# A fused attention and token-mixing kernel: when the queries and keys of two batches are loaded

## The chip, the cores and the metric

The kernel runs on one core of a Trainium2 chip. A core has a matrix engine (TensorE, in the profile PE, with its weight loads as PEld), a vector engine (VectorE, DVE), an activation engine (ScalarE, ACT), GpSimd (POOL) and SyncE (SP). GpSimd, SyncE and ScalarE also issue transfers, which a set of 16 DMA engines carries out. The metric is the device time of one execution in microseconds (us).

## The reference, cut to what matters

Four batches of attention (8 heads, 768 tokens, 64 channels a head) with a band of 96 local tokens and 8 global ones, followed by a layer that mixes tokens and channels. Everything is float32.

```python
# attention, per batch b and head h
scores = (q @ k.T) / sqrt(64) + bias      # bias: -slope_h * distance
scores = where(is_global | is_local, scores, -1e9)
a = softmax(scores)
x[b, :, h*64:(h+1)*64] = a @ v            # x is (4, 768, 512)
# the layer behind it, per batch
theta = x @ w_theta
zr, zi = x * cos(theta), x * sin(theta)
y = w_tok_r @ zr + w_tok_i @ zi           # over the 768 tokens
u = x + y
out = u + maximum(u @ w_ch, 0)
```

## The kernel before

The queries q, keys k and values v are loaded by GpSimd's queue, which also casts them to bfloat16. A buffer `qk` holds the q and k of one batch; there are two such buffers, so batch 3 takes the one that batch 1 leaves. The same holds for `vn` and v.

```python
ld = ctx.enter_context(tc.tile_pool(name="ld", bufs=2))
...
def alloc_qk(b):
    loads[b] = [ld.tile([T, 2, H, NT, D], BF, name="qk"), None]

def load_qk(b, h0, n, which=(0, 1)):           # rows of 6 tokens x 64 channels
    qk = loads[b][0]
    for i_ in which:
        nc.gpsimd.dma_start(
            out=qk[:, i_, h0:h0 + n].rearrange("p h t d -> p h (t d)"),
            in_=(q, k)[i_][b, h0:h0 + n].rearrange("h (p t) d -> p h (t d)", p=T))

def load_qk_tokens(b, h0, n):                  # one piece per head and tensor
    qk = loads[b][0]
    for h in range(h0, h0 + n):
        for i_ in range(2):
            pair = qk[:, i_, h // 2 * 2:h // 2 * 2 + 2].rearrange("p h t d -> p (h t d)")
            nc.gpsimd.dma_start(
                out=pair.rearrange("p (t h d) -> p t h d", t=NT, h=2)[:, :, h % 2],
                in_=(q, k)[i_][b, h].rearrange("(t p) d -> p t d", p=T))
```

Batches 0 to 2 are loaded by `load_qk`; batch 3 by `load_qk_tokens`, in an order in which a transposing DMA can turn a pair of heads without a copy ahead of it. Batches 1 and 2 need such a copy on VectorE and transposes on TensorE:

```python
def prep_copy(b, p):                           # batches 1 and 2
    ...
    with behind("dve"):
        for i_ in range(2):
            nc.vector.tensor_copy(
                out=qkn[:, :, i_].rearrange("p t h d -> p h t d"), in_=qk[:, i_, 2 * p:2 * p + 2])

def prep_dma(b, p):                            # batch 3: k and q of one pair of heads
    ...
    for i_ in (1, 0):
        to = qkT[(b, p)][i_] = att.tile([T, S], BF, name=("qT", "kT")[i_], bufs=6)
        with behind("sp"):
            nc.sync.dma_start_transpose(
                out=to.rearrange("p (t s) -> p t s", t=NT),
                in_=qk[:, i_, 2 * p:2 * p + 2].rearrange("p h t d -> p (h t d)"))
```

SyncE's queue carries three kinds of work in the order of the program: these transposes, the transposes of the attention's output x (`xtrans`) and of u (`utrans`) from batch 1 on, and the outputs (`chan`). `kglob` copies parts of a transposed k to `kG` on VectorE. The weights and the loads behind them:

```python
def load_w():
    nc.gpsimd.dma_start(out=w_theta_bf, in_=moe_w_theta.rearrange("(c p) n -> p c n", p=T))
    for tt in range(0, NT, 2):                 # NT = 6
        for wi, src in enumerate((moe_w_tok_r, moe_w_tok_i)):
            w2 = moe.tile([T, 2, S], BF, name="w_nat", bufs=6)
            nc.gpsimd.dma_start(
                out=w2, in_=src[tt * T:(tt + 2) * T, :].rearrange("(a p) s -> p a s", p=T))
            w_nat[wi, tt], w_nat[wi, tt + 1] = w2[:, 0], w2[:, 1]
        if tt == NT - 4:
            load_all_qk(1)
    nc.gpsimd.dma_start(out=w_ch_bf, in_=moe_w_ch.rearrange("(c p) n -> p c n", p=T))

def load_behind(b, tile):                      # called for batch 3 at the start of batch 1's layer
    g = nc.gpsimd.tensor_copy(out=gate, in_=tile).ins
    with tc.issue_after(g):
        alloc_qk(b)
        load_qk_tokens(b, 0, H)
        load_all_v(b)
...
load_w()
load_all_v(1)
load_all_qk(2)
```

The attention of batch b + 1 is woven into the token mixing of batch b, a step of `side` after so much of `main`:

```python
for b in range(B):
    ...
    if b == 2:
        order[:0] = [lambda p=p: prep_dma(3, p) for p in range(1, NP)]
    if b == 1:
        order.insert(0, lambda: load_behind(3, xT_sb[1][0:1, NC - 1, 0:1]))
    ...
    side = [(1536, f) for f in pre]            # pre: the preparation of batch 1, for b == 0
    if b == 0:
        side[:0] = [(0, lambda: load_all_v(2))]
        pass
    side += attention_steps(nxt, ahead) if nxt else []
    weave(main, side, 0.3 if b == 0 else 0.0, 0.9)
```

From the end of batch 0's attention on, the instructions of one engine are put in order by a scheduler, save where `behind` or a manual part fixes it.

Of the kernel before, what the change touches and what calls it, by code (L numbers as in the profile page):

```python
# [16 lines left out]
def kernel(  # L17
# [14 lines left out]
    B, H, S, D = q.shape  # L32
    T = 128
    NT = S // T
# [28 lines left out]
    def alloc_qk(b):  # L63
        loads[b] = [ld.tile([T, 2, H, NT, D], BF, name="qk"), None]

    def alloc_v(b):
        vn = loads[b][1] = ld.tile([T, H, NT, D + 1], BF, name="vn")
        nc.vector.memset(vn[:, :, :, D:D + 1], 1.0)  # L68

    def load_qk(b, h0, n, which=(0, 1)):  # L70
# [6 lines that stand above are left out]
    def load_qk_tokens(b, h0, n):  # L77
# [8 lines that stand above are left out]
    def load_v(b, h0, n):  # L86
        vn = loads[b][1]
        nc.gpsimd.dma_start(out=vn[:, h0:h0 + n, :, 0:D].rearrange("p h t d -> p (h t) d"),  # L88
                            in_=v[b, h0:h0 + n].rearrange("h (t p) d -> p (h t) d", p=T))
# [63 lines left out]
    def load_w():  # L153
        nc.gpsimd.dma_start(out=w_theta_bf, in_=moe_w_theta.rearrange("(c p) n -> p c n", p=T))
        for tt in range(0, NT, 2):
            for wi, src in enumerate((moe_w_tok_r, moe_w_tok_i)):
                w2 = moe.tile([T, 2, S], BF, name="w_nat", bufs=6)
                nc.gpsimd.dma_start(
                    out=w2, in_=src[tt * T:(tt + 2) * T, :].rearrange("(a p) s -> p a s", p=T))
                w_nat[wi, tt], w_nat[wi, tt + 1] = w2[:, 0], w2[:, 1]  # L160
            if tt == NT - 4:
                load_all_qk(1)
        nc.gpsimd.dma_start(out=w_ch_bf, in_=moe_w_ch.rearrange("(c p) n -> p c n", p=T))

    def trans_w(tt, copy=nc.vector.tensor_copy):
# [70 lines left out]
    def prep(b, p):  # L236
        if p == 0:
            prep_copy(b, 0)
        if p + 1 < NP:
            prep_copy(b, p + 1)  # L240
        qkn = qkns[b, p]
        qT = att.tile([T, S], BF, name="qT", bufs=6)
        kT = att.tile([T, S], BF, name="kT", bufs=6)
        for i_, dst in ((0, qT), (1, kT)):
            ps = ps_small([T, NT, T], BF)
            with behind("pe"):
                for t_ in range(NT):
                    nc.tensor.transpose(ps[:, t_, :], qkn[:, t_, i_].rearrange("p h d -> p (h d)"), ident)  # L248
            dst = dst.rearrange("p (n t) -> p n t", t=NT)
            src = ps.rearrange("p t n -> p n t")  # L250
            if i_ == 0:
                nc.vector.tensor_copy(out=dst, in_=src)  # L252
            else:
                nc.scalar.copy(out=dst, in_=src)

        qkT[(b, p)] = [qT, kT, None]
        kglob(b, p)

    def prep_dma(b, p):
        qk = loads[b][0]  # L260
        qkT[(b, p)] = [None, None, None]
# [6 lines that stand above are left out]
# [117 lines left out]
    def theta(b, c, j):  # L385
        last0 = [(j_, NC - 1) for j_ in range(2)]
        part = {0: [(0, dc) for dc in range(NC - 1)],
                1: [(1, dc) for dc in range(NC - 1)] + last0,
                2: [(j_, dc) for j_ in range(2) for dc in range(NC - 1)],
                3: last0}[j]  # L390
        if c == 0 and j in (0, 2):
            zri[b] = moe.tile([T, 2, NT, DM], BF, name="zri", tag="zri", bufs=1)
        xT, xb = xT_sb[b], x_sb[b]
        last = c == NT // 2 - 1
        if j in (0, 2):
            pss["th", c] = [ps_small([T, DM], FP) for _ in range(2)] if last else ps_big()
        pb = pss["th", c]
        st = lambda j_: slice((2 * c + j_) * T, (2 * c + j_ + 1) * T)
        for j_, dc in part:
            nc.tensor.matmul(pb[j_] if last else pb[:, j_, :], lhsT=xT[:, dc, st(j_)],  # L400
                             rhs=w_theta_bf[:, dc, :], start=(dc == 0), stop=(dc == NC - 1))
        if j in (1, 3):
            cs = moe.tile([T, 2, 2, DM], BF, name="cs")
            for i_, bias in ((0, {"bias": halfpi}), (1, {})):
                for o, p_ in [(cs[:, i_, j_], pb[j_]) for j_ in range(2)] if last else [(cs[:, i_], pb)]:
                    nc.scalar.activation(o, p_, AF.Sin, **bias)  # L406
            for i_ in range(2):
                for j_ in range(2):
                    nc.vector.tensor_mul(  # L409
                        zri[b][:, i_, 2 * c + j_, :].rearrange("p (g d) -> p g d", g=NP),  # L410
                        xb[:, :, 2 * c + j_, :],
                        cs[:, i_, j_].rearrange("p (g d) -> p g d", g=NP))
# [45 lines left out]
    def load_all_qk(b):  # L458
        alloc_qk(b)
        load_qk(b, 0, 8)  # L460

    def load_all_v(b):
        alloc_v(b)
        load_v(b, 0, 8)
# [4 lines left out]
    def load_behind(b, tile):  # L469
        g = nc.gpsimd.tensor_copy(out=gate, in_=tile).ins  # L470
        with tc.issue_after(g):
            alloc_qk(b)
            load_qk_tokens(b, 0, H)
            load_all_v(b)

    def attention_steps(b, preps):
# [25 lines left out]
    def weave(main, side, s0=0.0, s1=1.0):  # L502
# [11 lines left out]
        while i_ < len(side):  # L514
            side[i_][1]()
            i_ += 1

    load_w()
    load_all_v(1)
    load_all_qk(2)  # L520
    alloc_x(0)
# [80 lines left out]
    for b in range(B):  # L602
        nxt = b + 1 if b + 1 < B else None
        lag = 3
        th = [lambda c=c, j=j: theta(b, c, j) for c in range(NT // 2) for j in range(2)]
        pre = [lambda p=p: prep(1, p) for p in range(NP)] if b == 0 else []
        ahead = [[lambda p=p: prep(2, p) for p in range(NP)], [lambda p=p: prep_dma(3, p) for p in range(1)],
                 [], []][b]
        order = rest[:1] + th[:4] + rest[1:2] + th[4:] + rest[2:] if b else []
# [4 lines that stand above are left out]
        for f in order:  # L614
            f()
        main = []
        for tt in range(NT):
            for g in range(NT // 2):
                if (b, tt) != (B - 1, NT - 1):
                    main.append((2048, lambda tt=tt, g=g: mix(b, tt, g)))  # L620
                if b == 0 and g == 1 and tt + 1 < NT:
                    main.append((1536, lambda tt=tt: trans_w(tt + 1)))
                if tt >= lag and g == 0 and (b, tt) != (B - 1, NT - 1):
                    main.append((2048, lambda tt=tt: chan(b, tt - lag)))
                if b == 0 and tt and g == 1:
                    main.append((512, lambda tt=tt: utrans(b, tt - 1)))
            if b and (b, tt) != (B - 1, NT - 1):
                main.append((0, lambda tt=tt: utrans(b, tt)))
        side = [(1536, f) for f in pre]
        if b == 0:  # L630
            side[:0] = [(0, lambda: load_all_v(2))]
            pass
        side += attention_steps(nxt, ahead) if nxt else []
        weave(main, side, 0.3 if b == 0 else 0.0, 0.9)
        rest = [lambda tt=tt, b=b: chan(b, tt) for tt in range(NT - lag, NT)]
        if b == 0:
            rest.insert(1, lambda b=b: utrans(b, NT - 1))
# [44 lines left out]
```

The softmax here doesn't subtract the row's maximum and nothing guards it: scores larger than these inputs give would overflow.

## Time and profile before

| | us |
|---|---|
| time, median of three runs | 177.21 |
| lowest and highest | 177.1 and 177.56 |
| span of the profiled execution | 175.5 |
| TensorE busy | 160.7 |
| VectorE busy | 125.7 |
| ScalarE busy | 99.3 |
| GpSimd's DMA queue, share of 16 engines' span | 79.0% |
| SyncE's DMA queue, share of 16 engines' span | 33.5% |

The page divides the span into 40 slices of 4.39 us and gives each engine's busy share of a slice as a digit in tenths; the row named DMA is the mean of the 16 DMA engines. A row of waits reads: engine and line that waited, what ended the wait, the total in us, how often, the longest. A row of a timeline reads: start and duration in us, engine, line, operation, output and input, how many in a row. L12 is line 12 of the kernel. Busy time of TensorE is modelled from pipelined products, so a full row doesn't mean that it works at its peak.

### The profile page before, as it was taken

The page shows a single profiled execution, that of the slowest core. Times are in us where ns is not written, and L with a number is a line of the kernel's source. Part 1 is how long each engine was busy: PE and PEld are TensorE (multiplying, and loading weights), DVE is VectorE, ACT ScalarE, POOL GpSimd, SP SyncE. Part 2 cuts the span into 40 slices and gives each one's busy share as a digit, 9 for nine tenths or more (in the row PEclk, how much of TensorE's full clock was granted, in tenths as well). Part 3 has the DMA queues.
Part 4 walks back from the last instruction along what each step waited for, and adds up shares of the span by engine and source line. Part 5 has one row for each costly group of instructions (what it writes and reads, how often), then busy time and mean ns, then how long its engine had stood idle before and what let it go on. Part 6 is the DMA issues. An engine that isn't in the chain of part 4 may idle for free.

```text
span 175.5 us, 3752 instructions
## 1 busy us (share of the span) xinstructions
PE 160.7 (92%) x1534; PEld 83.9 (48%) x1534; DVE 125.7 (72%) x286; ACT 99.3 (57%) x127; POOL 38.0 (22%) x45
## 2 busy tenths in 40 slices
PE   7489789899999999999999996889999999999991
PEld 2355455345756566544455552333554644444440
DVE  5737676678999999997768786088877865724442
ACT  4698583999497694389933810669545508500010
POOL 8965346005000000299940000000000000000000
PEclk9999999999999999999999999999999999999999
DMA  5999999999999942399999997878254384314335
GB/s 154 198 172 179 213 204 203 207 206 166 168 204 166 150 119 49 105 133 163 176 129 151 94 240 171 147 134 227 76 105 106 91 147 124 120 37 107 99 90 181
DMA packets 75089, 25.94 MB, mean 148 GB/s; under 512 B 63168, under 2 KB 72128, under 8 KB 75072
## 3 DMA queue, kind: packets, MB, share of 16 engines
q0 software_dynamic: 45680, 12.45, 79.0%
q1 hardware_dynamic: 28976, 12.72, 33.5%
q10 hardware_dynamic: 416, 0.52, 0.9%
q8 instruction: 12, 0.20, 0.5%
q14 instruction: 5, 0.04, 0.1%
HBM read 25.69 MB, written 6.29 MB: 182 GB/s over the span
## 4 chain that ended last, share of the span: by engine, by line
PE 56%; DVE 17%; ACT 10%; DMA 9%; POOL 3%; issue 2%; SPq 1%; DVEq 0%; ACTq 0%; POOLq 0%
PE ps L420 27%; PE ps L448 9%; DMA vn<-in_v_dram 7%; ACT cs L406 6%; PE pb L400 6%; PE pb L357 4%; PE pb L298 3%; POOL qk L73 2%; ACT e L308 2%; DMA kT<-qk 2%; DVE qT L252 2%; PE ps L400 2%; DVE e L317 2%; DVE x_sb L368 2%; PE ps L248 2%
## 5 line engine op out<-in xcount | busy, mean ns | idle before, releaser
L420 PE MATMUL ps<-zri,w_tokT 128*128 128x512 bf16 x288 | 71.2, 379 | 1.6 <-DVE zri L409 0.7
L308 ACT ACTIVATE e<-pb 128x1024 bf16<-128x1024 f32 (+1 forms) x48 | 43.6, 959 | 20.6 <-PE pb L298 20.1
L420 PEld LDWEIGHTS <-w_tokT 128*128 128x128 bf16 x288 | 26.1, 98 | 30.4 <-issue 2.6
L425 DVE TENSOR_TENSOR u<-x_sb,ps 128x512 bf16<-128x512 bf16 x24 | 16.4, 682 | 13.1 <-PE ps L420 13.1
L448 PE MATMUL ps<-w_ch_bf,uT 128*128 128x512 bf16 (+1 forms) x100 | 24.7, 371 | 0.0
L409 DVE TENSOR_TENSOR zri<-x_sb,cs 128x512 bf16<-128x512 bf16 x48 | 18.1, 420 | 5.2 <-ACT cs L406 4.8
L406 ACT ACTIVATE cs<-pb,halfpi 128x1024 bf16<-128x1024 f32 x8 | 8.9, 1115 | 21.0 <-PE pb L400 21.0
L453 DVE SCALAR_TENSOR_TENSOR o_sb<-ps,u 128x512 f32<-128x512 f32 (+1 forms) x25 | 16.5, 665 | 3.1 <-PE ps L448 3.1
L400 PE MATMUL pb<-w_theta_bf,xT 128*128 128x512 bf16 x64 | 15.5, 379 | 2.2 <-DMA xT<-x_sb 2.2
L298 PE MATMUL pb<-qT,kT 64*128 64x128 bf16 x224 | 15.7, 219 | 1.9 <-DVE qT L213 1.3
L317 DVE TENSOR_TENSOR e<-e,etab 128x1024 bf16<-128x1024 bf16 (+1 forms) x24 | 14.7, 616 | 3.6 <-ACT e L308 3.5
L298 PEld LDWEIGHTS <-kT 64*128 64x128 bf16 x224 | 9.1, 93 | 15.3 <-issue 12.6
L400 PEld LDWEIGHTS <-xT 128*128 128x128 bf16 x96 | 9.0, 98 | 13.1 <-DMA xT<-x_sb 3.6
L439 ACT COPY uT<-ps 128x512 bf16<-128x512 bf16 x7 | 4.1, 587 | 18.6 <-PE ps L438 18.6
L357 PEld LDWEIGHTS <-e 128*128 128x128 bf16 x352 | 12.7, 97 | 3.9 <-issue 1.7
L448 PEld LDWEIGHTS <-uT 128*128 128x128 bf16 x100 | 9.2, 98 | 10.0 <-ACT uT L439 0.8
L298 PE MATMUL pb<-qT,kG 64*128 64x128 bf16 x128 | 12.0, 217 | 0.7 <-DVE kG L224 0.4
L88 POOL DMA_DIRECT2D vn<-in_v_dram x5 | 9.7, 1940 | 12.0 <-DVE vn L68 10.3
L368 DVE TENSOR_TENSOR x_sb<-pb,rec 128x768 bf16<-128x768 f32 x12 | 11.4, 949 | 0.3
L320 DVE TENSOR_TENSOR e<-e,etab 128x1024 bf16<-128x1024 bf16 x12 | 8.2, 685 | 2.9 <-ACT e L308 2.9
L222 DVE COPY kG<-kT 128x512 bf16<-128x512 bf16 x15 | 4.2, 282 | 8.0 <-DMA kT<-qk 5.8
L357 PE MATMUL pb<-vn,e 128*128 128x65 bf16 x168 | 9.6, 193 | 0.0
(73 smaller groups left out, 204.9 us busy)
## 6 DMA issues: line engine op xcount, KB each, us to landing
out_dram<-o_sb SPq DMA_DIRECT2D x23, 256.0 KB, 2.4
vn<-in_v_dram POOLq DMA_DIRECT2D x3, 768.0 KB, 22.3
qk<-in_q_dram POOLq DMA_DIRECT2D x2, 768.0 KB, 21.0
qk<-in_k_dram POOLq DMA_DIRECT2D x2, 768.0 KB, 24.0
w_nat<-in_moe_w_tok_r_dram POOLq DMA_DIRECT2D x3, 384.0 KB, 15.6
w_nat<-in_moe_w_tok_i_dram POOLq DMA_DIRECT2D x3, 384.0 KB, 15.1
vn<-in_v_dram POOLq DMA_DIRECT2D x2, 384.0 KB, 10.1
qk<-in_q_dram POOLq DMA_DIRECT2D x8, 96.0 KB, 4.8
```

Of the source, the lines that this page charges most:

```text
L298: nc.tensor.matmul(pb[:, hh, o:o + T], lhsT=lhsT, rhs=qT[R, (own, nxt)[part]], start=bool(b), stop=bool(b) or (jt == NT - 1 or (j == 1 and ...
L308: ins = nc.scalar.activation(e_c, pb[:, :, 0:n], AF.Exp, scale=scale).ins
L317: nc.vector.tensor_mul(e_c, e_c, tab[:, :, s0:s0 + n // T].rearrange("p a s n -> p a (s n)"))
L357: nc.tensor.matmul(o, lhsT=l_, rhs=r_, start=(i_ == 0), stop=(i_ == len(mms) - 1))
L368: nc.vector.tensor_mul(xv, po4[:, :, :, 0:D], rec.to_broadcast([T, n, nt, D]))
L400: nc.tensor.matmul(pb[j_] if last else pb[:, j_, :], lhsT=xT[:, dc, st(j_)], rhs=w_theta_bf[:, dc, :], start=(dc == 0), stop=(dc == NC - 1))
L406: nc.scalar.activation(o, p_, AF.Sin, **bias)
L409: nc.vector.tensor_mul(zri[b][:, i_, 2 * c + j_, :].rearrange("p (g d) -> p g d", g=NP), xb[:, :, 2 * c + j_, :], cs[:, i_, j_].rearrange( ...
L420: anchor["pe"] = nc.tensor.matmul(ps, lhsT=w_tokT[wi][:, st, tt * T:(tt + 1) * T], rhs=zri[b][:, wi, st, :], start=(st == 0 and wi == 0), ...
L425: anchor["dve"] = nc.vector.tensor_add(u_sb[b, tt].rearrange("p (g d) -> p g d", g=NP), x_sb[b][:, :, tt, :], ps.rearrange("p (g d) -> p g ...
L448: nc.tensor.matmul(ps_c, lhsT=uT[:, dc, :], rhs=w_ch_bf[:, dc, i_ * n:(i_ + 1) * n], start=(dc == 0), stop=(dc == NC - 1))
L453: nc.vector.scalar_tensor_tensor(o_sb[:, cols], in0=ps_c, scalar=0.0, in1=u[:, cols], op0=ALU.max, op1=ALU.add)
```

## The change

Two loads move.

- The q and k of batch 1 were issued between the second and the third pair of token-weight loads; now they follow all weights.
- The q and k of batch 3 (16 pieces, one per head and tensor) were all issued at the start of batch 1's layer, ahead of v of batch 3. Now the eight pieces of heads 0 to 3 are issued while batch 0's layer runs, behind the preparation of batch 1, whose buffer they take; the eight pieces of heads 4 to 7 and v stay where they were.

No computation is added or removed and no transfer changes its size. The first move lets the weights pass ahead of data that is needed later; the second spreads batch 3's small pieces over two stages, so that fewer transfers share the DMA engines with the transposes of batch 1.

```diff
@@ load_w
                 w_nat[wi, tt], w_nat[wi, tt + 1] = w2[:, 0], w2[:, 1]
-            if tt == NT - 4:
-                load_all_qk(1)
         nc.gpsimd.dma_start(out=w_ch_bf, in_=moe_w_ch.rearrange("(c p) n -> p c n", p=T))
@@ load_behind
         with tc.issue_after(g):
-            alloc_qk(b)
-            load_qk_tokens(b, 0, H)
+            load_qk_tokens(b, H // 2, H // 2)
             load_all_v(b)
@@
     load_w()
+    load_all_qk(1)
     load_all_v(1)
     load_all_qk(2)
@@ the loop over batches
         if b == 0:
             side[:0] = [(0, lambda: load_all_v(2))]
-            pass
+            side.append((0, lambda: (alloc_qk(3), load_qk_tokens(3, 0, H // 2))))
         side += attention_steps(nxt, ahead) if nxt else []
```

## The prediction, made before the changed kernel was run

> **What bounds the kernel now.** I read the page first: engine shares, then the forty slices.
>
> ```profile
> PE 160.7 (92%) x1534; PEld 83.9 (48%) x1534; DVE 125.7 (72%) x286; ACT 99.3 (57%) x127; POOL 38.0 (22%) x45
> ...
> PE   7489789899999999999999996889999999999991
> PEld 2355455345756566544455552333554644444440
> DVE  5737676678999999997768786088877865724442
> ACT  4698583999497694389933810669545508500010
> POOL 8965346005000000299940000000000000000000
> PEclk9999999999999999999999999999999999999999
> DMA  5999999999999942399999997878254384314335
> ```
>
> TensorE is busy 160.7 of 175.5 us at the full clock, so no change of loads can bring more than the 14.8 us in which it is idle. One slice is 4.39 us. Idle time sits at the start, in slices 24 and 25 (105 to 114 us, the start of batch 2's channel phase), and at the end. VectorE is at 9 from slice 10 to 17 (44 to 79 us): there it is the second bound, and a late input shows at once. The DMA row stands at 9 until 61 us, falls to 4, 2, 3 from 61 to 75, and is at 9 again from 75 to 105. The change moves transfers between exactly these stretches.
>
> Next, busy time by stage, for the two stages concerned (columns after the length: PE, PEld, DVE, ACT, POOL busy):
>
> ```profile
> 40.00:60.00 20.00, 19.75 (x244) 12.02 (x241) 19.60 (x45) 15.06 (x20) 1.88 (x1) 1.00 2.35 177
> ...
> 100.00:120.00 20.00, 16.91 (x128) 7.99 (x127) 12.82 (x31) 9.04 (x13) 0.00 (x0) 1.00 0.90 170
> ```
>
> From 40 to 60 us both PE and DVE are full; from 100 to 120 us PE loses 3.1 us. The waits from 104 to 117 us say to what:
>
> ```profile
> DVE kG L222 <- DMA kT<-qk: 5.8, 1, 5.8
> PEld L400 <- DMA xT<-x_sb: 3.2, 2, 2.1
> PE pb L400 <- DMA xT<-x_sb: 2.2, 2, 1.6
> ```
>
> PE waits 0.6 and 1.6 us for the transposed x of batch 2 and, lower in the same view, 0.7 us for a VectorE that had stood 5.8 us in a wait for batch 3's transposed k. Both come off SyncE's queue, so the last view is its timeline there (start, duration):
>
> ```profile
> 95.26 2.33 SPq L372 DMA_TRANSPOSE xT<-x_sb  x1
> 97.68 1.81 SPq L455 DMA_DIRECT2D out_dram<-o_sb  x1
> 99.59 2.11 SPq L265 DMA_TRANSPOSE kT<-qk  x1
> 101.80 1.23 SPq L265 DMA_TRANSPOSE qT<-qk  x1
> 103.14 1.21 SPq L434 DMA_TRANSPOSE uT<-u  x1
> 104.44 0.53 SPq L455 DMA_DIRECT2D out_dram<-o_sb  x1
> 105.06 1.25 SPq L372 DMA_TRANSPOSE xT<-x_sb  x1
> 106.41 1.21 SPq L434 DMA_TRANSPOSE uT<-u  x1
> 107.71 1.24 SPq L372 DMA_TRANSPOSE xT<-x_sb  x1
> ```
>
> The queue has no pause from 95.26 us on. The issue at 95.26 us comes when its input is ready, so the backlog begins there. A transpose takes 1.23 us to issue when undisturbed and an output 0.53; the first three take 2.33, 1.81 and 2.11. That is 1.10 + 1.28 + 0.88 = 3.3 us of lengthening, all while v of batch 3 is still arriving: issued at 87.4, landed 14.8 us later, at 102.2 us. The last x of batch 2 is ready at 104.6 (VectorE's timeline) but is issued at 107.71: 3.1 us of queue.
>
> **What the Trainium skill says.** "DMA: Bandwidth & Descriptors", section "Issuing engines are not separate DMA queues": transfers of every issuing engine share 16 DMA engines and interleave. The trace agrees: v(3) on GpSimd's queue and the transposes on SyncE's slow each other; the first transposed k landed 4.8 us after issue, the later ones alone after 2.8. The same page, "Why small descriptors are slow (HBM only)": packets carry a fixed cost. Token pieces write about 126 B a packet at some 32 ns, the plain q and k loads about 755 B at some 78 ns: per byte the pieces cost 2.5 times as much, so it matters beside what they run. "SBUF — State Buffer", section "Who interferes with whom": VectorE's copies in its two-port modes and GpSimd exclude each other. The trace agrees on a small scale: when batch 3's pieces start to be issued, one 128x32 kG copy takes 0.51 us instead of 0.15 to 0.17, and the second issue 1.38 instead of 0.82.
>
> **The change, part by part.**
>
> *Batch 1's q and k behind the weights.* The bytes do not change, only the order. Landings before, from issue plus landing time: fourth w_nat 28.3, q(1) 32.0, k(1) 35.9, last two w_nat 37.8 and 39.7, w_ch 42.3, v(1) 48.4. The steps are 3.8 us for q or k, 1.9 for a w_nat, 2.6 for w_ch: the queue runs first in, first out and never starves. In the new order: w_nat 30.2 and 32.1, w_ch 34.7, q(1) 38.4, k(1) 42.3, and v(1) still 48.4. GpSimd's issue times do not bind: its waits fit a window of eight transfers in flight (the issue at 19.09 follows the landing of the second half of v(0) at 18.81, eight before it), so q(1) is issued at about 21 and k(1) at 23. The first copy of q(1) runs at 41.98 us and that of k(1) about 0.3 us later, at 42.3. The 6 us of slack that k(1) had are spent to the last tenth. I charge **+0.3 us**: VectorE is full there, so any wait is lost. Weights gain nothing: w_ch is first used at 50.4, the last w_tok transposes at 63.6.
>
> *Half of batch 3's q and k in batch 0.* Eight pieces (heads 0 to 3) go behind v(2) on GpSimd's queue. Their buffer is batch 1's, free after its last copy at 46.4 us. At 0.82 us an issue most can go at once, but their packets stand behind v(2), which lands at 62.0 us. At the 151 KB/us that the queue moves in such packets when full, 98 KB take 0.65 us; eight take 5.2, so they land by about 68 us, in the valley of the DMA row. They meet the transpose of x(1) at 66.50; with the worst landing seen (4.8 us instead of 2.9) it would be there at 71.3, and PE uses it at 72.2: hidden. The last x(1) is issued at 70.45, after them. Descriptor writing beside VectorE's copies: the sixteen issues of before lengthen some copies by about 0.5 us in sum; half of that, in a stretch where VectorE is the bound: **+0.3 us**.
>
> *What leaves batch 1.* The gate still opens at 73.24, but only eight pieces follow, so v(3) is issued at about 87.4 - 8 x 0.83 = 80.8 instead of 87.4 us. The eighth piece, issued at 80.1, lands some 4.1 us later (as those issued near 80 us did), at 84.2; v(3) then needs between 6.6 us (v(2) behind k(2): 62.0 - 55.4) and 9.5 (before: 92.7 to 102.2). It lands at 90.8 to 93.7, before SyncE's backlog begins at 95.26.
>
> *What that is worth.* With undisturbed durations I replay SyncE's queue: 95.26 x, 96.6 output, 97.2 k, 98.5 q, 99.8 u, 101.1 output, 102.3 x (now when ready), 103.6 u, 104.9 x. The last x(2) is issued 2.8 us earlier and lands 2.8 us later, at 107.7 instead of 110.5. PE, which reaches these products at 106.65, then waits some 0.3 us instead of 2.25; the second k(3) comes about 3 us earlier, so VectorE leaves its wait sooner and the 0.66 us of PE goes too. Full sum: 2.25 + 0.66 - 0.3 = 2.6 us. But an instruction fetch falls at 97 us, and packets are also slow just after one at 112 us, when no load runs; and the k issued at 110.99 takes 2.42 us with no load beside it. So part of the 3.3 us was not v(3)'s doing; I take off a tenth: **-2.3 us**.
>
> Sum: -2.3 + 0.3 + 0.3 = -1.7 us, 177.2 - 1.7 = **175.5 us**. From 120 us on PE is nearly full and nothing is changed, so what PE wins by 117 us should reach the end.
>
> **Rivals.** *A wait for k(1) takes the place of the one removed.* For it: the slack of 0.0 us, and a VectorE and PE full from 42 to 60 us. If q(1) and k(1) come 2 us later than my order says, the whole gain is spent: 177.3. If the scheduler, which orders instructions outside the manual parts by readiness as it estimates it, also puts these copies behind others, PE could starve: 179. Against it: the last byte of the same set of transfers lands at the same 42.3. *The slow issues are not v(3)'s doing* but that of the instruction fetch and of transposes on each other. For it: the 2.42 us just named. Against it: three in a row are long only while v(3) is in flight. Then only some 0.6 us is won and the costs stay: 177.2. *A freer stretch is worth more than the wait:* u and x transposes between 84 and 95 us land earlier too, and the order shifts favourably; with no cost in batch 0 that makes -3.5 us: 173.7. Against it: PE is busy 19.81 of 20 us from 80 to 100.
>
> **Range and chances.** Full gain without costs gives 174.6, the rivals 173.7 and 177.2 to 179. Eight in ten between **173.3 and 178.0 us**. 2% is 3.5 us, more than all the idle time that I know how to remove from 100 to 120 us: faster **0.11**, within 2% **0.81**, slower **0.08** (for the late k(1) with a bad order).
>
> **What would show it.** Right: the DMA row filled at 61 to 68 us and no longer at 9 after about 96; v(3) landing before 95; the three issues near 95 to 100 us at 1.2, 0.5 and 1.2; VectorE's wait for kT shorter by about 3 us and PE's loss from 100 to 120 below 1. Wrong: a wait of VectorE for q(1) or k(1) near 42 us; long issues near 97 us with no load in flight; the instructions of PE or VectorE in another order, above all between 42 and 75 us. Then the time is set by the schedule and not by these transfers.

## The result, and the profile after

The changed kernel takes **174.86 us** (median of four runs, 174.38 to 175.26) against 177.16 for the one before: a ratio of 0.987, 95% interval 0.983 to 0.991. The forecast was 175.5 us, the range 173.3 to 178.0. The order of the instructions on TensorE, VectorE, ScalarE and SyncE's queue is the same in both traces, one by one; only the loads on GpSimd stand elsewhere. So the two timelines can be laid on each other.

From the page of the changed kernel, TensorE's and the DMA engines' busy tenths in forty slices (now 4.31 us each):

```profile
PE   7699989899999999999999999989999999999991
...
DMA  4999999999999999999999677889245372323335
```

The valley of the DMA row at 61 to 75 us is filled, and the row falls below 9 from 95 us on instead of 105. TensorE's dip at 105 to 114 us is nearly gone. Busy time by stage in the changed kernel, columns as before:

```profile
40.00:60.00 20.00, 19.79 (x238) 11.75 (x237) 19.60 (x45) 14.64 (x20) 7.26 (x8) 1.00 2.35 175
...
100.00:120.00 20.00, 19.22 (x150) 9.18 (x147) 15.02 (x34) 11.82 (x15) 0.00 (x0) 1.00 0.80 171
```

From 100 to 120 us PE (TensorE) loses 0.8 us instead of 3.1; the stage from 40 to 60 us is as full as it was. The waits of the changed kernel from 104 to 117 us (who, for what, total, times, longest):

```profile
DVE kG L220 <- DMA kT<-qk: 3.1, 1, 3.1
...
PEld L398 <- DMA xT<-x_sb: 0.2, 1, 0.2
```

PE's own waits for the transposed x, 0.6 and 1.6 us before, are gone (the weight loads keep one of 0.2), and VectorE's wait for k has come down from 5.8 to 3.1 us. The reason stands in SyncE's timeline of the changed kernel (start, duration):

```profile
93.28 2.09 SPq L432 DMA_TRANSPOSE uT<-u  x1
95.46 1.24 SPq L370 DMA_TRANSPOSE xT<-x_sb  x1
96.80 0.53 SPq L453 DMA_DIRECT2D out_dram<-o_sb  x1
97.43 1.24 SPq L263 DMA_TRANSPOSE kT<-qk  x1
...
104.69 1.24 SPq L370 DMA_TRANSPOSE xT<-x_sb  x1
```

The three issues that took 2.33, 1.81 and 2.11 us take 1.24, 0.53 and 1.24. The last x of batch 2 goes out at 104.69 instead of 107.71. And v of batch 3 is in place before this backlog: its load, in GpSimd's timeline of the changed kernel, and how long it took to land:

```profile
79.93 2.26 POOL L88 DMA_DIRECT2D vn<-in_v_dram  x1
```

```profile
DMA to landing us min/median/max: 13.2/13.2/13.2
```

What that is worth stands in TensorE's timelines, the one before first and the changed one below it (in brackets the idle time ahead of an instruction, and what ended it):

```profile
113.55 1.89 PE L400 MATMUL ps<-w_theta_bf,xT 128*128 128x512 bf16 x8
116.97 1.02 PE L420 MATMUL ps<-zri,w_tokT 128*128 128x512 bf16 x4 [0.66 <-DVE o_sb L453]
```

```profile
110.68 1.89 PE L398 MATMUL ps<-w_theta_bf,xT 128*128 128x512 bf16 x8
113.92 1.02 PE L418 MATMUL ps<-zri,w_tokT 128*128 128x512 bf16 x4 [0.48 <-DVE o_sb L451]
```

The first products that use x of batch 2 begin at 106.37 us instead of 106.65, a lead of 0.28 us. At the last of them, the first row of each view, the lead is 2.87 us, and one wait later 3.05: **2.77 us** are won in this stretch, and the lead stays to the end (3.13). The two profiled executions lie further apart than the medians (2.3 us): the one before was the slowest of its four, the one after the fastest of its four.

### The profile page after: what moved, and what is told of

Read it like the earlier page. It is cut to its first block, busy times and chain, and to the rows that moved or that the text cites. A ratio compares the mean times of both kernels' runs of the same rounds, so it can differ in the third digit from the quotient of the medians.

```text
span 172.4 us, 3753 instructions
## 1 busy us (share of the span) xinstructions
PE 162.2 (94%) x1534; PEld 84.7 (49%) x1534; DVE 126.3 (73%) x286; ACT 99.3 (58%) x127; POOL 37.4 (22%) x45
## 4 chain that ended last, share of the span: by engine, by line
PE 61%; DVE 19%; ACT 12%; DMA 5%; issue 1%; DVEq 0%; ACTq 0%; SPq 0%
PE ps L418 28%; PE ps L446 9%; ACT cs L404 6%; PE pb L398 6%; PE pb L296 5%; PE pb L355 4%; ACT e L306 3%; DMA qk<-in_k_dram 3%; DVE x_sb L366 2%; DMA kT<-qk 2%; DVE qT L250 2%; PE ps L398 2%; DVE e L315 2%; PE pb L276 2%; PE ps L246 2%; ACT L306 1%
## 5 line engine op out<-in xcount | busy, mean ns | idle before, releaser
L398 PEld LDWEIGHTS <-xT 128*128 128x128 bf16 x96 | 9.2, 98 | 10.1 <-DMA xT<-x_sb 0.2
L88 POOL DMA_DIRECT2D vn<-in_v_dram x5 | 9.6, 1923 | 12.3 <-DVE vn L68 10.7
L252 ACT COPY kT<-ps 128x768 bf16<-128x768 bf16 x8 | 6.4, 798 | 5.5 <-PE ps L246 5.5
```

## The experiments

The theory: the gain comes from v of batch 3 being gone before SyncE's backlog begins near 95 us. Its rivals: the order of batch 1's q and k has a part in it, or the long issues come of instruction fetches, or any freer stretch helps. The kernels ran on several chips; all ratios and all differences to the kernel before are to its median on the same chip (176.95 to 177.30 us). "Queue empty" is the last landing of GpSimd's loads; "lengthening" is what the nine SyncE issues from the first to the last x of the backlog took beyond 1.23 us (0.53 for an output). In e9 to e12 it holds an output that met an instruction fetch (1.1, 0.6, 1.0 and 0.9 us). All columns but the last two are read from one profiled execution. The traces of e1 to e4, e11 and e12 lack the records of 25 products that the others have, so some tenths of the idle time of PE in these rows (up to 0.5 us from 60 to 80 us) aren't real.

| kernel | queue empty | lengthening | wait for kT | PE idle 60-80, 100-120 | time | ratio (interval) |
|---|---|---|---|---|---|---|
| before | 102.2 | 3.3 | 5.8 | 0.3, 3.1 | 177.16 | 1 |
| after | 93.1 | 0.1 | 3.1 | 0.3, 0.8 | 174.86 | 0.987 (0.983 to 0.991) |
| e1 first move alone | 102.4 | 3.1 | 5.6 | 0.7, 2.9 | 177.37 | 1.001 (0.998 to 1.003) |
| e2 second move alone | 92.9 | 0.0 | 2.9 | 0.8, 0.7 | 174.94 | 0.988 (0.984 to 0.992) |
| e3 after, spare loads | 101.8 | 1.8 | 4.3 | 0.9, 1.8 | 176.16 | 0.995 (0.993 to 0.997) |
| e4 sixteen pieces | 89.1 | 0.0 | 3.1 | 4.0, 0.6 | 178.60 | 1.009 (1.005 to 1.012) |
| e5 before, v earlier | 101.7 | 2.9 | 5.1 | 0.2, 2.5 | 176.32 | 0.996 (0.994 to 0.999) |
| e6 four pieces | 94.9 | 0.5 | 2.8 | 0.3, 0.5 | 174.60 | 0.986 (0.982 to 0.989) |
| e7 twelve pieces | 90.7 | 0.1 | 3.2 | 1.2, 0.9 | 176.32 | 0.996 (0.993 to 0.998) |
| e8 after, v earlier | 93.3 | 0.1 | 2.9 | 0.4, 0.6 | 174.70 | 0.987 (0.983 to 0.991) |
| e9 before, fetches moved | 103.9 | 3.8 | 4.6 | 0.3, 2.7 | 176.96 | 0.999 (0.997 to 1.001) |
| e10 after, fetches moved | 94.0 | 0.7 | 2.4 | 0.5, 0.3 | 174.38 | 0.984 (0.981 to 0.987) |
| e11 second move, fetches moved | 93.1 | 1.1 | 2.8 | 0.8, 0.6 | 174.16 | 0.984 (0.982 to 0.987) |
| e12 the same, four pieces | 96.0 | 0.9 | 2.6 | 0.7, 0.4 | 173.74 | 0.983 (0.980 to 0.986) |

### One move at a time

The first move alone, to the kernel before:

```diff
-            if tt == NT - 4:
-                load_all_qk(1)
...
     load_w()
+    load_all_qk(1)
     load_all_v(1)
```

> Only batch 1's q and k go behind the weights; batch 3 is loaded as before. Theory (the gain is in the freed SyncE queue near 95 to 102 us, and this move is free at best): v(3) still lands near 102 us, the issues at 95 to 100 us stay near 2.3, 1.8 and 2.1 us, VectorE's wait for kT stays near 5.8 us, and the time is that of before, 177.2 us, within 0.4. Rival (the first move brings a part itself, since the profile after is already 0.43 us ahead from 23 us on and v(0) lands about 0.9 us earlier): 0.5 to 1 us faster, 176.2 to 176.7, with v(0)'s second half landing before 18 us. Second rival (k(1) late): slower by 0.3 us or more, with a wait of VectorE's copy for k(1) near 42 us.

Measured: 177.37 us, a ratio of 1.001 with an interval that holds 1. The second half of v(0) landed 11.0 us after its issue, before in 11.7: across all fourteen kernels it takes 10.1 to 12.3 us, 10.9 to 12.3 with the old order of loads and 10.1 to 11.9 with the new. So the 0.4 us by which the profile after was ahead at 23 us is of the size of the spread between executions. This move by itself has no effect that shows; the interval leaves room for 0.3 us won to 0.5 us lost.

The second move alone:

```diff
-            alloc_qk(b)
-            load_qk_tokens(b, 0, H)
+            load_qk_tokens(b, H // 2, H // 2)
             load_all_v(b)
...
+            side.append((0, lambda: (alloc_qk(3), load_qk_tokens(3, 0, H // 2))))
```

> Only half of batch 3's pieces go to batch 0; batch 1's q and k stay between the weights. Theory: the whole gain is here. v(3) lands near 93 us, the three issues near 95 to 100 us take 1.2, 0.5 and 1.2 us, VectorE's wait for kT falls from 5.8 to 3.1 us, PE's loss from 100 to 120 us falls from 3.1 to 0.8, and the time is 174.8 us within 0.5. Rival (the first move brings a part): 175.5 to 176.5.

Measured: 174.94 us, the changed kernel's time. Within the intervals the whole gain is in the second move.

### Put the traffic back

```diff
             load_qk_tokens(b, H // 2, H // 2)
             load_all_v(b)
+            for h in (0, H // 2):
+                spare = moe.tile([T, 2, S], BF, name="w_nat", bufs=6)
+                nc.gpsimd.dma_start(
+                    out=spare.rearrange("p a s -> p (a s)").rearrange("p (n d) -> p n d", d=D),
+                    in_=v[b, h:h + H // 2].rearrange("h (t p) d -> p (h t) d", p=T))
```

> The changed kernel with two further loads of half of v(3) each into buffers that nobody reads, issued behind v(3): as many small packets as v(3) itself, so the queue of GpSimd is busy again until about 101 us. Everything else is the changed kernel, in the same order. Theory (packets of that queue lengthen SyncE's issues): at least two of the three issues near 95 to 100 us are longer again by 0.8 us or more, the last x of batch 2 is issued 2 to 3 us later than in the changed kernel, VectorE's wait for kT is back to 5 to 6 us, and the time goes back to 176.5 to 177.6 us. Rival (the long issues came of the instruction fetch and of transposes on each other): the issues stay at 1.2, 0.5 and 1.2 us outside the fetch, and the time stays within 0.4 us of 174.9.

Measured: 176.16 us. Against before, that is 1.1 us won where the changed kernel wins 2.3: about half is given back. The timeline of SyncE in this kernel (in an execution of 177.14 us, the second slowest of 22):

```profile
95.94 1.21 SPq L370 DMA_TRANSPOSE xT<-x_sb  x1
97.24 0.53 SPq L453 DMA_DIRECT2D out_dram<-o_sb  x1
97.88 3.04 SPq L263 DMA_TRANSPOSE kT<-qk  x1
```

One issue is long, by 1.8 us, and not two or more as I expected; the two ahead of it are short although the spare loads were under way. So not every issue beside traffic is long. As v(3) itself was in place by 94.0 us, what came back is not a wait for v. But the long k also met an instruction fetch, which began at 98.8 us in this kernel and at 94.0 in the changed one. So this run alone doesn't tell the spare packets from the fetch; the runs with moved fetches below do.

### How much to move

The changed kernel with another number of pieces in batch 0; for sixteen:

```diff
-            load_qk_tokens(b, H // 2, H // 2)
             load_all_v(b)
...
-            side.append((0, lambda: (alloc_qk(3), load_qk_tokens(3, 0, H // 2))))
+            side.append((0, lambda: (alloc_qk(3), load_qk_tokens(3, 0, H))))
```

> The changed kernel with all sixteen pieces in batch 0, so that only v(3) is left at the start of batch 1's layer; it lands near 83 us. Theory (what counts is that v(3) is gone before SyncE's backlog begins at 95 us, and PE is full from 80 to 100): no further gain there, 174.9 within 0.4; the pieces now run until about 74 us beside both last transposes of x of batch 1, which may land up to 2 us later; if PE meets that, at most 0.5 to 1 us slower. Rival (a freer stretch from 84 to 95 us is worth something by itself): another 0.5 to 1 us faster, 174.0 to 174.4.

Measured: 178.60 us, 3.7 more than with eight, where I had allowed 1. The gain near 100 us is there (no lengthening, wait for kT 3.1 us) but more is lost earlier. The waits from 68 to 80 us, and below them, from the view of the tile xT on SyncE's queue from 56 to 75 us, how long its four transposes took to land:

```profile
PEld L398 <- DMA xT<-x_sb: 4.0, 2, 2.1
...
PE pb L398 <- DMA xT<-x_sb: 3.1, 2, 1.6
```

```profile
DMA to landing us min/median/max: 7.5/8.1/8.2
```

In the changed kernel the last of these landed after 2.7 us. Beside the pieces, of which the last landed at 78.6 us and not at 74, it took 7.5, and TensorE waited for two of them: a transfer that was hidden with eight pieces ends the path with sixteen. (The order of the instructions is the same here and with twelve, save one MEMSET of 0.1 us on VectorE.) With four and with twelve (`2` and `6` heads in the diff above):

> The changed kernel with four pieces in batch 0 instead of eight, twelve left in batch 1. Theory: v(3) is issued near 83.3 us and lands near 97.5, inside SyncE's backlog, so part of the long issues stays: 175.5 to 176.6 us, between before (177.2) and after (174.9); no wait of PE for x of batch 1. Rival (some transfer out of the way is enough): 174.9 within 0.4.

> The changed kernel with twelve pieces in batch 0 instead of eight. Theory, from the run with all sixteen, in which the last three transposes of x of batch 1 took 7.5 to 8.2 us to land beside the pieces and PE waited for them: the third lands some 6 to 8 us after issue, the last one later than 2.7 but less than 7.5 us, PE waits 0.5 to 2.5 us for them between 70 and 80 us, and v(3) is gone before 90 us. The time is 175.4 to 177.4 us. Rival (the loss with sixteen came of the later gate or of GpSimd's issues beside VectorE): it stays at 174.9 within 0.4, or loses without a wait of PE for x.

Measured with four: 174.60 us, as good as eight. v(3) was issued at 83.5 us and landed at 94.9, not at 97.5, just ahead of the backlog; so the expectation missed by its landing time, and the rule behind it held here. With twelve: 176.32 us; the third x took 6.9 us to land, the last 4.2, and PE waited 0.9 us for x (another 0.4 us were VectorE's wait for k of batch 1). Between four and eight pieces the time is flat, and both ends of the choice have their own wait.

### Empty the queue sooner by order alone

```diff
-            load_qk_tokens(b, 0, H)
-            load_all_v(b)
+            load_all_v(b)
+            load_qk_tokens(b, 0, H)
```

> The kernel before, with one change: at the start of batch 1's layer v of batch 3 is issued ahead of the sixteen pieces and not behind them; nothing moves to batch 0. The pieces alone are issued every 0.82 us but need only 0.65 us of the queue, so before the queue idled between them and then had v left at the end; with v first the pieces pile up behind it. Theory (what counts is when GpSimd's queue is empty, not how much it carries in this stage): the queue is empty near 94 to 96 us instead of 102, most of the long issues near 95 to 100 us go, and the time is 174.8 to 175.8 us. Rival (the amount in this stage counts, and only moving pieces to another stage helps): 176.8 us or more.

Measured: 176.32 us, 0.7 better, not 2. The edit did not do what I thought. Three pieces still went ahead of v (why the scheduler put them there isn't shown). Then, behind a piece issued at 82.95 us, GpSimd stopped for 4.81 us (its timeline in this kernel):

```profile
88.66 0.82 POOL L82 DMA_DIRECT2D qk<-in_q_dram  x1 [4.81 <-DMA vn<-in_v_dram]
```

The load eight before this one is v, which landed at 88.4 us, just ahead of it: as in the trace before, eight loads were in flight at most. The last piece landed at 101.7 us, hardly earlier than before, and two issues were long: k with 3.03 us, which met a fetch at 95.9 us, and q with 2.26, which met none. So the run does not refute that the time of emptying counts, but it tests it only in part. The same edit to the changed kernel:

> The changed kernel with v of batch 3 issued ahead of the eight pieces that are left in batch 1. Theory: the queue is empty near 88 to 90 us instead of 93, well before the backlog, which was empty-handed already: 174.9 within 0.4, perhaps 0.2 us better since the transposes of u near 85 to 93 us meet less. Rival (a freer stretch from 84 to 95 us is worth something by itself): 174.4 us or less.

Measured: 174.70 us. The queue was empty at 93.3 us and not at 88 to 90: three pieces again went ahead of v, v landed at 88.8, and the other five landed behind it. So the stretch was no freer than in the changed kernel, and this run tests the rival hardly at all. e4 does, with a queue empty at 89.1 us: against the trace before, VectorE wins 2.8 us there between the instructions of 106 and of 115 us, as with eight pieces, and nothing between those of 85 and 104.

### Move the instruction fetches

The trace shows twelve fetches of 16 KB of instructions in a queue of their own; one began at 97.2 us before and at 94.0 after. Before, it ran for 1.8 us, so the output of 1.81 us lay mostly inside it, the long x mostly ahead of it and the long k behind it. To move them, small products are added where TensorE idles:

```diff
+    def idle(ps, n):
+        for _ in range(n):
+            nc.tensor.matmul(ps[:, 0:16], lhsT=zero[:, 0:T], rhs=zero[:, 0:16], start=True, stop=True)
...
     score_bias(0, 1)
+    idle(spare, 30)
...
     turn0(0, 0)
+    idle(spare, 30)
```

Here `spare` is the tile that `warm` writes. To the kernel before:

> The kernel before with 60 more small products (16 columns of a zero tile, result unused) on TensorE in the two gaps of over 1 us that it has before 8.2 us. They add no time there but 120 instructions, so that the 16 KB instruction fetch that fell at 97 us, among the long issues, comes some 5 to 7 us of work earlier (near 88 to 91 us), and the one after it near 103 to 106. All loads are as before: v(3) still lands near 102 us. Theory A (packets of GpSimd's queue alone lengthen SyncE's issues): no change, at least two long issues between 95 and 101 us, 177.2 within 0.5. Theory B (only the fetch, meeting that queue while both are busy, does it): the issues near 95 to 101 us fall to 1.2, 0.5 and 1.2 us, VectorE's wait for kT to about 3 us, and the time to 174.8 to 175.6 us although the loads are those of before.

Measured: 176.96 us, a ratio of 0.999. The fetches went to 92.3 and 104.5 us, and the issues stayed long, in SyncE's timeline of this kernel:

```profile
95.74 2.64 SPq L377 DMA_TRANSPOSE xT<-x_sb  x1
98.47 0.54 SPq L460 DMA_DIRECT2D out_dram<-o_sb  x1
99.12 1.78 SPq L270 DMA_TRANSPOSE kT<-qk  x1
101.00 1.94 SPq L270 DMA_TRANSPOSE qT<-qk  x1
...
104.38 1.62 SPq L460 DMA_DIRECT2D out_dram<-o_sb  x1
```

With no fetch from 93 to 104 us the first, third and fourth lose 1.4, 0.5 and 0.7 us. Theory B falls: beside the load, issues are long without a fetch. To the changed kernel:

> The changed kernel with the same 60 small products. v(3) lands near 93 us, ahead of SyncE's backlog, so both theories expect short issues near 95 to 101 us and 174.9 us within 0.5; it shows what the products and the shifted fetches cost by themselves. A theory A difference between this run and the one before it: 2.3 us; theory B: below 0.7 us.

Measured: 174.38 us; the difference to e9 is 2.6 us, as theory A has it. The fetches do have a share of their own. The k issued at 108 to 112 us took 2.42 us before and 2.30 after, with a fetch beside it; in both e9 and e10, where that fetch comes 7 us earlier, it takes 1.23, and the output that now meets the fetch takes 1.62 and 1.14 instead of 0.53. So a fetch lengthened these issues by 0.6 to 1.2 us. It adds to the load's effect and doesn't replace it: e10 has a fetch inside the backlog and is as fast as the changed kernel.

This run also shows the cost that the first move can have, in its waits from 40 to 46 us:

```profile
DVE qkn L236 <- DMA qk<-in_k_dram: 1.1, 1, 1.1
```

### The second move with the products

The second move without the first, with the products of e10:

> Second move alone (eight pieces in batch 0, batch 1's q and k between the weights as before) and the 60 small products. In the run of the changed kernel with these products VectorE waited 1.1 us for k of batch 1, which the first move makes late. Theory: without the first move that wait is gone, the rest stays, so the time is 0.3 to 1.1 us below that run: 173.3 to 174.1 us. Rival (something else ends at the same time): 174.4 within 0.3. If the products cost by themselves: above 174.9.

> As the run before it, with four pieces in batch 0 instead of eight. v(3) lands near 95 us, at the edge of SyncE's backlog, and the transposes of x of batch 1 meet fewer pieces. Theory: the same as with eight within 0.4 us, as long as v(3) lands ahead of the backlog; if it lands after it, up to 1 us slower.

Measured: 174.16 and 173.74 us. The wait for k(1) is gone in both, and the profiled execution of e11 is 0.8 us shorter than that of e10 (172.1 and 172.9 us), but the ratios to before (0.984 and 0.983) do not differ from e10's 0.984 beyond their intervals. The best time measured is e12's, 1.7% (1.4 to 2.0) below before; that it beats the changed kernel is likely by the medians but not separated, as the two intervals overlap (0.980 to 0.986 and 0.983 to 0.991). In e12 v(3) landed at 96.0 us, 1.0 us after the backlog had begun, and nothing was lost: so the moment by which v must be gone is not a sharp one.

## Why the prediction was right, step by step

**What leaves batch 1, and its worth.** v(3) was to be issued at 80.8 us and to land at 90.8 to 93.7; it was issued at 79.9 and landed at 93.1. The replay of SyncE's queue gave 96.6, 97.2, 98.5, 99.8, 101.1, 102.3, 103.6 and 104.9; the trace has 96.80, 97.43, 98.78, 100.11, 101.41, 102.03, 103.39 and 104.69. The worth was put at 2.6 us and cut to 2.3 for the fetch; the stretch from 106 to 115 us brought 2.77. That the full sum is so near is partly luck, since two of its terms were off against each other. The products that use x were to win 2.25 - 0.3 = 1.95 us; they won 2.87 - 0.28 = 2.59, as no wait for x was left. The 0.66 us of TensorE behind VectorE were to go too; 0.48 of them stayed, so this term won 0.18. The cut for the fetch was not needed: in the changed kernel the fetch began at 94.0 us, on a u transpose ahead of the backlog (the 2.09 above), and cost the path nothing. The prediction had not foreseen that it would come 3 us earlier, and why it did, with no instruction added, is not shown.

**Half of batch 3 in batch 0: hidden, but by less than I wrote.** The pieces were to land by 68 us. The last one landed at 70.7 (61.72 + 8.94), so eight took 9.2 us from the landing of v(2) at 61.4 and not 5.2. The 151 KB/us of the prediction are about what all queues together moved in this time (150), transposes among them; the eight pieces, 786 KB in 9.2 us, got 85. The third x(1) took 5.2 us to land and was there at 71.4, 0.6 us ahead of its use at 71.95. The 4.8 us that I called the worst landing were not the worst of the trace before: beside v(3) the first two x of batch 2 took 10.5 and 7.7 us there. That x(1) stayed hidden with eight pieces was thus less sure than the prediction made it; e7 and e4 show how close it was. Two smaller readings of the trace before were off by 0.5 us without effect: the piece issued at 80.08 landed 4.7 us later, and the last of the sixteen at 92.2.

**Descriptor writing beside VectorE.** Charged 0.3 us. VectorE's lead over the trace before shrinks by 0.15 us between 45 and 48 us, where two kG copies take 0.43 and 0.34 us instead of 0.28 and 0.17. But that is one execution: between 44 and 55 us the profiles of e2, e3, e6, e8, e11 and e12, all with pieces in batch 0 and none with a wait for k(1), lose 0.15 to 0.53 us against the trace before, and those of e1, e5 and e9, without such pieces, lose none. So 0.3 was a fair charge, if the writing is the cause of this loss.

**Batch 1's q and k.** Charged 0.3 us. k(1) landed at 41.5 us (predicted 42.3) and its copy ran at 41.8: no wait in the profiled run. e1 shows no cost (1.001), but its interval would also hold the 0.3. The slack is as thin as was said: e4, e7 and e10, which reach that point early, wait 0.6, 0.4 and 1.1 us.

**The sum.** -2.3 + 0.3 + 0.3 gave -1.7 us; measured by the medians is -2.3. The mechanism was the one named. The term that was mis-sized is the gain, 2.77 us in the profiles where 2.3 was put; the costs (0.15 and 0 in the profile of the changed kernel) are too small to be told from the spread.

**The rivals.** A late k(1) took nothing from this kernel, but is real in others. A freer stretch from 84 us on is worth nothing that e4 shows. That the long issues were the fetch's doing is refuted as their main cause by e9 and right for a part: the output of 1.81 us before.

## What to carry to other kernels

Before moving a load, look for the queue whose issues run late one behind another, find the first long issue, and ask which transfer is in flight there: here it was enough to have that transfer gone by about then, and more bought nothing. Then ask the same of the place to which the load moves: sixteen pieces won the same wait, and lost 3.7 us between 68 and 80 us to transposes that had been hidden. In this kernel the choice is flat from four to eight pieces, with a loss on either side.

## What the runs showed of the hardware that I had not expected

- The issue of a transposing DMA by SyncE, 1.23 us when undisturbed, took up to 2.64 us (e9) while loads of small packets were under way on another engine's queue, and up to 3.04 us where a fetch came on top (e3); the whole queue behind it waits. Others beside the same traffic stayed at 1.21 (e3), so it comes in bursts. In e9, from 95 to 102 us and with no fetch, 27 single packets of the two queues took over 0.3 us, up to 0.85, where the median is 0.03. What makes a burst is not settled.
- A fetch of instructions lengthened the SyncE issue that it met by 0.6 to 1.2 us (before, after, e9, e10), and 60 added products moved it: the one at 111.7 us before came 7 us earlier in e9.
- The landing of a transposing DMA suffers more than its issue: 2.7 us alone, 7.5 to 8.2 beside the sixteen pieces of e4, while its issue took 1.2 to 1.3 us there, and 10.5 beside v(3) before.
